# A gated feed-forward block beside a state-space block on one core: the last gate tiles as half products inside an output pair, and three differences by negated copy and DMA

## The chip, the core and the metric

The kernel runs on one core of a Trainium2 chip. The engines named here are PE (TensorE, matrix products; its weight loads are listed as PEld), DVE (VectorE), ACT (ScalarE), POOL (GpSimd, which here mostly issues transfers that add into their target) and SP (SyncE, which issues loads and stores). PE reads SBUF and writes PSUM; DVE and ACT read and write both. Each engine works through its own list of instructions in order and waits for the others by semaphores. The metric is the time of one execution on the device in microseconds (us); less is better.

## The reference

The input x has 2048 tokens of width 512. It is normalized per token, and the result is

```python
xn = _layernorm(x)
# A: a diagonal complex recurrence over the tokens, 512 states
h = Lam_bar[None, :] * h + Bu[:, t, :]                 # for t in 0..2047
y = 2.0 * jnp.einsum("blp,dp->bld", hseq, Cmat).real + xn * Dskip
# B: a gated feed-forward block, 512 -> 1792 -> 512
out_B = (silu(xn @ w1) * (xn @ w3)) @ w2
out = x + y + out_B
```

So there are three groups of matrix products: xn with w1 (gate) and w3 (up), xn with the state weights B, and a last one in which the products silu(gate)*up (1792 wide, 14 tiles of 128) and the states (real and imaginary, 8 tiles) meet w2 and C.

## The kernel before

**Blocks.** The 2048 tokens are four blocks of 512 (blocks 0 to 3). For each block the kernel makes the gate and up tiles (14 each, 128 features by 512 tokens), the state inputs (4 tiles, real and imaginary), rotates and scans the state inputs along the tokens on DVE (`ssm_tasks`: `pre_a`, `pre_b`, `pre_c`, then eight scans in two halves `hf`, then `post_a`, `post_b`, `post_c`), and writes gates and states as float16 into the tile `act`, which holds 22 tiles of 128 rows per token chunk. Where `pre_c` or `post_c` adds two large tiles, it either runs on DVE (L493, L525) or is an adding transfer that POOL issues (L495, L527).

**Output pairs.** `act` is multiplied with [w2; C] in eight output pairs, numbered 0 to 7; pair n belongs to block n // 2 and covers two chunks of 128 tokens. Each pair (`y_fast`, L1036) is a 2x2 block product by seven instead of eight half products (the scheme of Strassen and Winograd). Each half product is 11 matmuls of 128x256 (L1054). The left sides are a11, a12, a22 from `act` and four sums, S1 = a21 + a22, S3 = a11 - a21, S2 = S3 - a22 and S4 = a12 + S2, made ahead by `row_sums` (L993): S3 and S2 by DVE subtractions of 128x1408 (L1000), S1 by DVE or an adding transfer (L1005, L1007), S4 by DVE or a transfer inside the pair (L1093 to L1096). S2 and S3 of pair n live in `homes[n % 2]`. The half products of pairs 4, 5 and 6 run in the order 1, 4, 2, 6, 5, 7, 3; in pairs 4 and 5 the third is put off and runs inside the following pair after that one's product 5. `seeds(n)` loads a pair's PSUM tiles with the residual by ACT.

**Block 3's up side.** The same scheme is used on the up side of the last block (`glu_last`, L837): tiles 0 to 11 are three groups of four, each group seven half products of four 128x256 matmuls (`product`, L867), accumulated in four PSUM tiles g, e (pool `ps_y`), f, z (pool `ps_bu`), with copies between them by ACT (L857) and adds by DVE (L879). Its left sums come from `up_sums` (L834), and one of them, `s4n`, is made inside the group (L910). The gate side of these groups is done plainly, one tile at a time: four matmuls of 128x512 (`side`, L848) and a Silu on ACT (`gate_side`, L860). Tiles 12 and 13 are plain on both sides. After that come pairs 4 to 7; the pairs of block 3 are 6 and 7.

**Who sets the order.** The order is written out by hand. DVE's background work (scans, posts, sums) stands in a list `bg` (`Filler`, L24), which keeps an estimate of PE's and DVE's time; `bg.fill()` emits tasks from the head of the list as long as the estimate of DVE is not too far ahead of PE's, and `bg.flush(key)` emits everything from the head up to the last task with that key. POOL and SP issue their transfers in the order of the program.

Of the kernel before, what the change touches and what calls it, by code (L numbers as in the profile page):

```python
# [63 lines left out]
def kernel(  # L64
# [397 lines left out]
    def ssm_tasks(b, posts_last=False, between=(), middle=(), late=()):  # L462
# [5 lines left out]
        def half(hf):  # L468
            psl = slice(2 * hf, 2 * hf + 2)
            st = {}  # L470

            def pre_a():
                if b == 0:
                    sin_step((2 * hf + 1, 1))
                    nc.vector.tensor_scalar(out=tabe[:, psl, 2, :], in0=tabe[:, psl, 1, :], scalar1=-1.0,
                                            scalar2=None, op0=ALU.mult)
                st["g"] = u_blk[b, hf]
                if (b, hf) == (3, 0):
                    st["p"] = up.tile(FULL, BF16, name="u")
                elif b == NBLK - 1:  # L480
                    st["p"] = xtp.tile([P, NDT, TBLK], BF16, name="xnT").rearrange("p (j r) t -> p j r t", r=2)
                else:
                    st["p"] = ssmw.tile(FULL, BF16, name="p")
                nc.vector.tensor_tensor(out=st["p"][:, :, ::-1, :], in0=st["g"], in1=tabe[:, psl, 2:0:-1, :],
                                        op=ALU.mult)

            def pre_b():
                nc.vector.tensor_tensor(out=st["g"], in0=st["g"], in1=tabe[:, psl, 0:1, :].to_broadcast(FULL),  # L488
                                        op=ALU.mult)

            def pre_c():
                if b == 0 or (b, hf) == (2, 0):
                    nc.vector.tensor_tensor(out=st["g"], in0=st["g"], in1=st["p"], op=ALU.add)  # L493
                else:
                    gp.dma_start(out=st["g"], in_=st["p"], accum_op=ALU.add)  # L495

            def scan(j, ri):
                pt = 2 * hf + j
                init = 0.0
                if b in (1, 2):  # L500
                    init = ends[:, hf, 2 * j + ri:2 * j + ri + 1]
                elif b > 2:
                    init = act_blk[b - 1][:, CPB - 1, k_state(pt, ri), P - 1:P]
                v = st["g"][:, j, ri, :]
                nc.vector.tensor_tensor_scan(out=v, data0=rho[:, pt:pt + 1].to_broadcast([P, TBLK]), data1=v,  # L505
                                             initial=init, op0=ALU.mult, op1=ALU.add)

            def post_a(csl=slice(0, CPB)):
                if "p16" not in st:
                    st["p16"] = ssmw.tile(FULL, BF16, name="p").bitcast(FP16).rearrange(  # L510
                        "p j r (c t) -> p (j r c t)", t=P).rearrange("p (c k t) -> p c k t", c=CPB, t=P)
                tsl = slice(csl.start * P, csl.stop * P)
                nc.vector.tensor_tensor(out=by_state(st["p16"][:, csl]), in0=by_chunk(st["g"][:, :, ::-1, tsl]),  # L513
                                        in1=by_chunk(tabe[:, psl, 2:0:-1, tsl]), op=ALU.mult)

            def post_b(csl=slice(0, CPB)):
                tsl = slice(csl.start * P, csl.stop * P)
                n = csl.stop - csl.start
                nc.vector.tensor_tensor(out=by_state(act_state(b, hf)[:, csl]), in0=by_chunk(st["g"][:, :, :, tsl]),  # L519
                                        in1=by_chunk(tabe[:, psl, 0:1, tsl]).to_broadcast([P, 2, 2, n, P]), op=ALU.mult)  # L520
# [16 lines left out]
        transfers = (post0[2],) + (() if b == NBLK - 1 else (post1[2],)) + ((pre1[2],) if b > 0 else ()) + ((pre0[2],) if b in (1, 3) else ())  # L537

        def add(*fns):
            for fn in fns:  # L540
# [285 lines left out]
    def up_sums(b):  # L826
# [8 lines left out]
                for out, x, z, op in ((s1, a21, a22, ALU.add), (s3, a11, a21, ALU.subtract),  # L835
                                      (s2, s1, a11, ALU.subtract))]

    def glu_last(b):
        xnT = xnT_blk[b]
        s1, s2, s3, s4 = ups["s"]  # L840
# [33 lines left out]
        def halves(ps):  # L874
            return ps.rearrange("p (h t) -> p h t", h=2)

        def add(out, ps):
            bg.own(0.7)
            nc.vector.tensor_tensor(out=out, in0=halves(ps), in1=halves(s5), op=ALU.add)  # L879

        gates = []
        for f in range(4 * NG, NFT):
# [6 lines left out]
                gates.pop()()  # L889
            if f % 2 == 1:  # L890
                gates.append(lambda f=f, tiles=tiles: gate(f - 1, tiles))
        for n in range(NG):
            f0 = 4 * n
            a11, a12, a22, s1n, s2n, s3n, s4n = (v[:, :, n, :] for v in (
                up_quarter(0, 0), up_quarter(1, 0), up_quarter(1, 1), s1, s2, s3, s4))
            g, e = (ps_y.tile([P, TBLK], FP32, name="y_ps") for _ in range(2))
            f, z = (ps_bu.tile([P, TBLK], FP32, name="bu_ps") for _ in range(2))
            upper, lower = pair_tiles(), pair_tiles()
            product(g, a11, b11, True)
            copy(f, g)  # L900
            product(e, s1n, t1, True)
            copy(s5, e)
            gate_side(f0, upper[0])
            bg.fill(0.8)
            gates.pop()()
            product(f, a12, b21, False)
            product(g, s2n, t2, False)
            copy(e, g)
            bg.own(0.42)
            nc.vector.tensor_tensor(out=s4n, in0=a12, in1=s2n, op=ALU.subtract)  # L910
            copy(upper[1][:, :, 0:TH], halves(f))
            gate_side(f0 + 1, upper[0])
            bg.fill()
            product(g, s3n, t3, False)
            copy(z, g)
            add(lower[1][:, :, TH:TBLK], g)
            product(e, s4n, b22, False)
            add(upper[1][:, :, TH:TBLK], e)
            gate_side(f0 + 2, lower[0])
            bg.fill()  # L920
            gate(f0, upper)
            product(z, a22, t4, False)
            copy(lower[1][:, :, 0:TH], halves(z))
            gate_side(f0 + 3, lower[0])
            bg.fill()
            gates.append(lambda f0=f0, lower=lower: gate(f0 + 2, lower))
        seeds(4)
        return gates.pop()


    def res_list(b):
# [56 lines left out]
        return [[v[:, 0:n] for v in xs], [spare[:, 0:n], spare[:, n:2 * n]]], q  # L988

    sums = {}  # L990

    def row_sums(n, b, p):
        a = act(b)  # L993
        a11, a12 = a[:, 2 * p, 0:NK, :], a[:, 2 * p, NK:2 * NK, :]
        a21, a22 = a[:, 2 * p + 1, 0:NK, :], a[:, 2 * p + 1, NK:2 * NK, :]
        s3, s2 = (v.bitcast(FP16).rearrange("p (k t) -> p k t", t=P) for v in homes[n % 2])
        sums[n] = dict(a11=a11, a12=a12, a22=a22, s1=a21, s2=s2, s3=s3)

        def subtract(out, x, z):
            return lambda: nc.vector.tensor_tensor(out=out, in0=x, in1=z, op=ALU.subtract)  # L1000

        three = (0.84, subtract(s3, a11, a21), ("sums", n))
        two = (0.84, subtract(s2, s3, a22), ("sums", n))
        if n in (1, 6, 7):
# [31 lines left out]
    def y_fast(n, then=(), between=()):  # L1036
# [50 lines left out]
        def product2():  # L1087
# [9 lines left out]
            add(o1[:, D1], f, o1[:, D1])  # L1097
            if last:
                store(c1, o1, D1)
            if n + 1 < len(pairs) and n not in (1, 2, 3) and n - 1 not in LATER:  # L1100
                seeds(n + 1)
            steps()

# [43 lines left out]
        for i in ((1, 5, 2, 6, 4, 3, 7) if b == 0 else (1, 2, 4, 6, 5, 7, 3) if b == 1 else ORDER.get(n, (1, 4, 2, 6, 5, 7, 3))):  # L1147
# [10 lines left out]
            if between:  # L1158
# [2 lines left out]
                    bg.fill()  # L1161
                if n == 3 and not between:
                    bg.first(up_sums(3))
            if n == 2 and i == 7:
                seeds(3)

    ln_alloc(0)
    ln1a, ln1b = ln_tasks_vector(1)
# [70 lines left out]
    y_done.append(2)  # L1239
    y_fast(3, (), bu_fast(3, 1))  # L1240
    bg.flush("up")
    gate = glu_last(3)
    gate()
    for n in range(4, len(pairs)):
        ahead = row_sums(n + 1, *pairs[n + 1]) if n + 1 < len(pairs) else ()
# [37 lines left out]
```

## Time and profile before

| | |
|---|---|
| median of 3 runs | 201.05 us (200.91 to 201.06) |
| span of the profiled execution, first to last instruction | 199.5 us |
| PE busy | 195.6 us (98%) |
| DVE busy | 181.8 us (91%) |
| ACT busy | 135.0 us (68%) |
| POOL busy | 51.5 us (26%) |
| plain matmul 128x512 of block 3 (L848), 64 of them | 16 take 3.45 us |
| half product of four 128x256 matmuls (L869) | 0.44 us |
| DVE scan of 128x512 (L505), 32 of them | about 1.27 us |
| granted TensorE clock, mean | 0.999 |

The profiled execution's own time is its span of 199.5 us; the page gives no other time for it, and the median of the runs, which also counts what lies before the first and after the last instruction, is 1.55 us longer. A timeline row is: start in us, duration in us, engine, source line, operation, output and input tiles with their shapes, count, and in brackets how long the engine was idle before it and what ended that. Rows of engines that overlap consecutive instructions have durations a little longer than the distance to the next start; where a step follows a step on the same engine, the distance of the starts is what counts. In the table by stretches each pair after the interval is busy us and count of instructions by engine, then the granted clock, the share of the DMA engines and GB/s.

### The profile page before, as it was taken

Reading aid. Unit: us, or ns where it says so; the run is one execution under the profiler, and the core shown is the slowest. Engines: PE = TensorE matmul, PEld = TensorE weight load, DVE = VectorE, ACT = ScalarE, POOL = GpSimd, SP = SyncE. Lnnn points to the kernel's source line nnn. Section 1 sums busy time; section 2 is a strip of 40 time slices with the busy share of each in tenths; the row PEclk is TensorE's granted clock in tenths of the full one; section 3 lists DMA queues with packets and bytes.
Section 4 is the critical chain, followed back from the end, with each engine's and each line's share of the span. In section 5 each row is a group of like instructions: output and inputs, shape, how many; then the busy total and the mean of one; then the engine's idle time right before and its main releaser. Section 6 shows DMA issues by size and latency. Waiting matters only on the chain.

```text
span 199.5 us, 3700 instructions
## 1 busy us (share of the span) xinstructions
PE 195.6 (98%) x1401; PEld 130.7 (65%) x1401; DVE 181.8 (91%) x254; ACT 135.0 (68%) x281; POOL 51.5 (26%) x75
## 2 busy tenths in 40 slices
PE   8999999999999999999999999999999999999994
PEld 2774444444444488866555468888566678888893
DVE  3689699999999999989999997999999999999972
ACT  4699897699999996968998684362588783111220
POOL 7180289700411134041202305040021303310000
PEclk9999999999999999999999999999999999999999
DMA  4999996991497054730997455838137732941111
GB/s 138 326 277 200 302 186 124 343 273 23 69 181 141 0 105 82 135 105 0 156 148 119 89 92 98 172 83 132 53 59 129 149 56 52 174 92 36 53 44 40
DMA packets 32258, 25.12 MB, mean 126 GB/s; under 512 B 16240, under 2 KB 29936, under 8 KB 32240
## 3 DMA queue, kind: packets, MB, share of 16 engines
q0 software_dynamic: 6128, 11.38, 33.5%
q1 hardware_dynamic: 25536, 13.21, 26.8%
q10 hardware_dynamic: 576, 0.30, 0.5%
q8 instruction: 11, 0.18, 0.4%
q14 instruction: 7, 0.06, 0.1%
HBM read 7.74 MB, written 2.10 MB: 49 GB/s over the span
## 4 chain that ended last, share of the span: by engine, by line
PE 95%; DMA 2%; SPq 1%; issue 0%; DVE 0%
PE gu_ps L587 34%; PE gu_ps L1054 17%; PE y_ps L1054 10%; PE gu_ps L848 7%; PE bu_ps L1054 7%; PE bu_ps L454 3%; PE y_ps L454 3%; PE y_ps L869 3%; PE y_ps L780 3%; DMA w_sb<-in_B_w_dram 2%; PE gu_ps L619 2%; PE gu_ps L780 2%; PE bu_ps L869 1%; PE bu_ps L780 1%; PE bu_ps L619 1%; SPq L166 0%
## 5 line engine op out<-in xcount | busy, mean ns | idle before, releaser
L587 PE MATMUL gu_ps<-xnT,w_sb 128*128 128x512 bf16 x312 | 69.6, 379 | 0.0
L587 PEld LDWEIGHTS <-w_sb 128*128 128x128 bf16 x312 | 30.5, 98 | 34.2
L1054 PEld LDWEIGHTS <-act 128*128 128x128 f16 x462 | 43.5, 98 | 5.4
L596 ACT ACTIVATE g<-gu_ps 128x512 bf16<-128x512 f32 x41 | 24.8, 606 | 6.0 <-PE gu_ps L587 3.6
L597 ACT ACTIVATE u<-gu_ps 128x512 bf16<-128x512 f32 x41 | 24.8, 606 | 4.5 <-PE gu_ps L587 3.7
L505 DVE TENSOR_TENSOR_SCAN u<-rho,ends,u 128x512 bf16<-128x512 f32 x16 | 20.0, 1270 | 0.0
L527 POOL DMA_DIRECT2D act<-p x7 | 9.2, 1320 | 34.0 <-DVE act L519 22.1
L1054 PE MATMUL gu_ps<-w_sb,act 128*128 128x256 bf16 (+3 forms) x126 | 16.0, 267 | 0.0
L848 PE MATMUL gu_ps<-xnT,w_sb 128*128 128x512 bf16 x64 | 15.9, 379 | 0.0
L604 DVE TENSOR_TENSOR act<-g,u 128x1024 f16<-128x1024 bf16 x21 | 14.2, 679 | 0.4 <-ACT u L597 0.4
L860 ACT ACTIVATE g<-gu_ps 128x512 bf16<-128x512 f32 x14 | 8.4, 599 | 5.4 <-PE gu_ps L848 5.0
L454 PEld LDWEIGHTS <-bt 128*128 128x128 bf16 x64 | 6.3, 98 | 7.5
L1077 ACT ACTIVATE x_blk<-gu_ps 128x256 f32<-128x256 f32 (+1 forms) x9 | 3.3, 368 | 10.6 <-PE gu_ps L1054 10.6
L1054 PE MATMUL bu_ps<-w_sb,act 128*128 128x256 bf16 (+3 forms) x84 | 10.4, 264 | 0.0
L1054 PE MATMUL gu_ps<-ct,act 128*128 128x256 f16 (+1 forms) x72 | 10.4, 267 | 0.0
L848 PEld LDWEIGHTS <-w_sb 128*128 128x128 bf16 x64 | 6.3, 98 | 4.8
L505 DVE TENSOR_TENSOR_SCAN u<-rho,u 128x512 bf16<-128x512 f32 x8 | 9.2, 1206 | 0.0
L1054 PEld LDWEIGHTS <-x_blk 128*128 128x128 f16 x88 | 8.6, 98 | 1.0
L1054 PEld LDWEIGHTS <-tw 128*128 128x128 f16 x88 | 8.6, 98 | 1.0
L513 DVE TENSOR_TENSOR p<-u,tabe 128x2048 f16<-128x2048 bf16 (+1 forms) x8 | 8.7, 1085 | 0.1
L519 DVE TENSOR_TENSOR act<-u,tabe 128x2048 f16<-128x2048 bf16 (+1 forms) x8 | 8.7, 1083 | 0.0
L488 DVE TENSOR_TENSOR u<-u,tabe 128x2048 bf16<-128x2048 bf16 x7 | 8.5, 1219 | 0.1
(203 smaller groups left out, 392.5 us busy)
## 6 DMA issues: line engine op xcount, KB each, us to landing
act<-p POOLq DMA_DIRECT2D x6, 512.0 KB, 6.1
xn<-x_blk POOLq DMA_DIRECT2D x4, 512.0 KB, 5.5
out_dram<-xn SPq DMA_DIRECT2D x15, 128.0 KB, 1.7
w_sb<-in_B_w_dram SPq DMA_DIRECT2D x1, 1792.0 KB, 8.2
act<-act POOLq DMA_DIRECT2D x5, 352.0 KB, 4.6
w_sb<-in_B_w_dram SPq DMA_DIRECT2D x2, 768.0 KB, 6.4
u<-p POOLq DMA_DIRECT2D x3, 512.0 KB, 5.1
w_sb<-in_B_w_dram SPq DMA_DIRECT2D x4, 256.0 KB, 4.9
```

The source lines that it names most:

```text
L454: nc.tensor.matmul(out=ps, lhsT=bt[:, ri, dt, pt * P:(pt + 1) * P], rhs=xnT_blk[b][:, dt, :], start=(dt == 0), stop=(dt == NDT - 1))
L505: nc.vector.tensor_tensor_scan(out=v, data0=rho[:, pt:pt + 1].to_broadcast([P, TBLK]), data1=v, initial=init, op0=ALU.mult, op1=ALU.add)
L513: nc.vector.tensor_tensor(out=by_state(st["p16"][:, csl]), in0=by_chunk(st["g"][:, :, ::-1, tsl]), in1=by_chunk(tabe[:, psl, 2:0:-1, tsl]) ...
L519: nc.vector.tensor_tensor(out=by_state(act_state(b, hf)[:, csl]), in0=by_chunk(st["g"][:, :, :, tsl]), in1=by_chunk(tabe[:, psl, 0:1, tsl] ...
L527: gp.dma_start(out=a, in_=p16, accum_op=ALU.add)
L587: nc.tensor.matmul(out=ps[:, tsl], lhsT=w[:, dt, f * P:(f + 1) * P], rhs=xnT[:, dt, tsl], start=(dt == 0), stop=(dt == NDT - 1))
L596: nc.scalar.activation(out=g16[:, f % 2, :], in_=g_ps, func=ACT.Silu)
L597: nc.scalar.activation(out=u16[:, f % 2, :], in_=u_ps, func=ACT.Copy)
L604: nc.vector.tensor_tensor(out=act_gates(b, f - 1), in0=split(g16), in1=split(u16), op=ALU.mult)
L780: nc.tensor.matmul(out=out[:, h * TH:(h + 1) * TH], lhsT=left[:, h, k, :], rhs=right[:, k, :], start=(start and h == 0 and k == 0), stop=( ...
L848: nc.tensor.matmul(out=ps, lhsT=w[:, dt, f * P:(f + 1) * P], rhs=xnT[:, dt, :], start=(dt == 0), stop=(dt == NDT - 1))
L1054: nc.tensor.matmul(out=out, lhsT=left[:, k, :], rhs=right[k][:, cols], start=(start and k == 0), stop=(k == NK - 1), skip_group_check=True)
```

## The change

The change has four parts.

- **Gate side of the third group by half products.** The four gate tiles of tile group 2 of block 3 (tiles 8 to 11) are no longer made by `gate_side`, but by the same seven half products as the up side. The new function `group` makes the seven steps for either side; for the gate side (`gated`) the results go through Silu, and the two DVE adds write back to PSUM first. The left sums of the gate side are made by the new `gate_sums` from w1 into space that group 0's up sums held (three DVE operations on 128x512 elements, key "gs"), added to the end of the list `bg` after group 0.
- **Where it runs.** Groups 0 and 1 stay in the loop, with plain gate tiles. Steps one and five of group 2's up side and the gate product of group 1's lower half run before pair 4; everything else of group 2, both sides, runs between the half products of pair 4 (six lists, one after each of pair 4's products 1, 4, 2, 6, 5, 7). The first gate step flushes the key "gs". `seeds(5)` moves from pair 4's product 2 to the end of pair 4.
- **S3 of pairs 4 and 5 and S2 of pair 5.** These are no longer DVE subtractions. ACT writes the negated subtrahend (128x1408, L1083), and POOL issues a transfer that adds the minuend (L1084). The first (S3 of pair 4) stands before group 0, the second (S3 of pair 5) inside group 0, the third (S2 of pair 5) before pair 4.
- **Block 2's first half.** Its `pre_c` becomes an adding transfer (L495) instead of a DVE add of 128x2048 (L493).

```diff
@@ ssm_tasks @@
-                if b == 0 or (b, hf) == (2, 0):
+                if b == 0:
                     nc.vector.tensor_tensor(out=st["g"], in0=st["g"], in1=st["p"], op=ALU.add)
                 else:
                     gp.dma_start(out=st["g"], in_=st["p"], accum_op=ALU.add)
@@ new @@
+    def gate_sums():
+        s1, s2 = (ups["s"][i][:, :, 0, :] for i in range(2))
+        a11, a12, a21, a22 = (gate_quarter(*i) for i in ((0, 0), (1, 0), (0, 1), (1, 1)))
+        s3, s4 = gate_quarter(0, 1, True), gate_quarter(1, 0, True)
+        ups["gs"] = a11, a12, a22, s1, s2, s3, s4
+        return [(0.42, lambda out=out, x=x, z=z, op=op: nc.vector.tensor_tensor(out=out, in0=x, in1=z, op=op), "gs")
+                for out, x, z, op in ((s1, a21, a22, ALU.add), (s3, a11, a21, ALU.subtract),
+                                      (s2, s1, a11, ALU.subtract))]
@@ glu_last: the seven steps @@
+        def group(lefts, four, top, low, gated):
+            a11, a12, a22, s1n, s2n, s3n, s4n = lefts
+            g, e = (ps_y.tile([P, TBLK], FP32, name="y_ps") for _ in range(2))
+            f, z = (ps_bu.tile([P, TBLK], FP32, name="bu_ps") for _ in range(2))
+            def end(out, ps):
+                nc.scalar.activation(out=out, in_=halves(ps), func=ACT.Silu if gated else ACT.Copy)
+            def add(out, ps):
+                bg.own(0.7)
+                nc.vector.tensor_tensor(out=halves(ps) if gated else out, in0=halves(ps), in1=halves(s5), op=ALU.add)
+                if gated:
+                    end(out, ps)
+            def one():
+                product(g, a11, b11, True)
+                copy(f, g)
+            def five():
+                product(e, s1n, t1, True)
+                copy(s5, e)
+            def two():
+                product(f, a12, b21, False)
+            def six():
+                product(g, s2n, t2, False)
+                copy(e, g)
+                four()
+                end(top[:, :, 0:TH], f)
+            def seven():
+                product(g, s3n, t3, False)
+                copy(z, g)
+                add(low[:, :, TH:TBLK], g)
+            def three():
+                product(e, s4n, b22, False)
+                add(top[:, :, TH:TBLK], e)
+            def last():
+                product(z, a22, t4, False)
+                end(low[:, :, 0:TH], z)
+            return one, five, two, six, seven, three, last
@@ glu_last: the order @@
-        for n in range(NG):
+        by_copy[4][0]()
+        for n in range(NG - 1):
...
+            one()
+            five()
             gate_side(f0, upper[0])
             bg.fill(0.8)
             gates.pop()()
+            two()
+            six()
             gate_side(f0 + 1, upper[0])
             bg.fill()
+            if n == 0:
+                by_copy[5][0]()
+            seven()
+            three()
             gate_side(f0 + 2, lower[0])
             bg.fill()
             gate(f0, upper)
+            last()
             gate_side(f0 + 3, lower[0])
             bg.fill()
             gates.append(lambda f0=f0, lower=lower: gate(f0 + 2, lower))
+            if n == 0:
+                for t in gate_sums():
+                    bg.add(*t)
         seeds(4)
-        return gates.pop()
...
+        def gate_step(i):
+            def run():
+                if "steps" not in state:
+                    bg.flush("gs")
+                    right = ups["gs"]
+                    state["steps"] = group(right, lambda: sums4(right[6], right[1], right[4]), upper[0], lower[0], True)
+                state["steps"][i]()
+            return run
+        one, five, two, six, seven, three, last = up_steps
+        gone, gfive, gtwo, gsix, gseven, gthree, glast = (gate_step(i) for i in range(7))
+        first = gates.pop()
+        return (one, five, first, by_copy[5][1]), deque(((two, six), (seven, three), (last, gone, gfive), (gtwo, gsix),
+                                          (gseven, gthree), (glast, lambda: gate(f0, upper), lambda: gate(f0 + 2, lower))))
@@ row_sums @@
+        def from_copy(out, x, z):
+            nc.scalar.activation(out=out, in_=z, func=ACT.Copy, scale=-1.0)
+            gp.dma_start(out=out, in_=x, accum_op=ALU.add)
+        by_copy[n] = [lambda: from_copy(s3, a11, a21), lambda: from_copy(s2, s3, a22)]
         three = (0.84, subtract(s3, a11, a21), ("sums", n))
         two = (0.84, subtract(s2, s3, a22), ("sums", n))
+        if n in (4, 5):
+            three = (0.0, lambda: None, ("sums", n))
+        if n == 5:
+            two = (0.0, lambda: None, ("sums", n))
@@ y_fast @@
-            if n + 1 < len(pairs) and n not in (1, 2, 3) and n - 1 not in LATER:
+            if n + 1 < len(pairs) and n not in (1, 2, 3, 4) and n - 1 not in LATER:
                 seeds(n + 1)
...
-            if n == 2 and i == 7:
-                seeds(3)
+            if n in (2, 4) and i == 7:
+                seeds(n + 1)
@@ the end @@
-    gate = glu_last(3)
-    gate()
+    sums5 = row_sums(5, *pairs[5])
+    begin, beside = glu_last(3)
+    for step in begin:
+        step()
+        bg.fill()
...
-        y_fast(n, ahead if n == 4 else ())
+        y_fast(n, ahead if n == 4 else (), beside if n == 4 else ())
```

More of the change, by code (lines that the diff above doesn't have):

```diff
@@ L535, in ssm_tasks @@
         (pre0, scans0, post0), (pre1, scans1, post1) = (half(hf) for hf in range(NPT // 2))
-        transfers = (post0[2],) + (() if b == NBLK - 1 else (post1[2],)) + ((pre1[2],) if b > 0 else ()) + ((pre0[2],) if b in (1, 3) else ())
+        transfers = (post0[2],) + (() if b == NBLK - 1 else (post1[2],)) + ((pre1[2],) if b > 0 else ()) + ((pre0[2],) if b > 0 else ())
         def add(*fns):
@@ L836, in up_sums, with gate_quarter @@
                                       (s2, s1, a11, ALU.subtract))]
+    def gate_quarter(kh, r, half=False):
+        f0 = 4 * (NG - 1) * P
+        v = w1_sb[:, 2 * kh:2 * kh + 2, f0 + r * 2 * P:f0 + (r + 1) * 2 * P]
+        return v.bitcast(FP16) if half else v
+    def gate_sums():
[6 more added lines that the diff above has]
+                                      (s2, s1, a11, ALU.subtract))]
     def glu_last(b):
@@ L875, in halves, with sums4, up_lefts @@
             return ps.rearrange("p (h t) -> p h t", h=2)
-        def add(out, ps):
-            bg.own(0.7)
-            nc.vector.tensor_tensor(out=out, in0=halves(ps), in1=halves(s5), op=ALU.add)
+        def group(lefts, four, top, low, gated):
[33 more added lines that the diff above has]
+            return one, five, two, six, seven, three, last
+        def sums4(out, x, z):
+            bg.own(0.42)
+            nc.vector.tensor_tensor(out=out, in0=x, in1=z, op=ALU.subtract)
+        def up_lefts(n):
+            return [v[:, :, n, :] for v in (up_quarter(0, 0), up_quarter(1, 0), up_quarter(1, 1), s1, s2, s3, s4)]
         gates = []
@@ L891, in glu_last @@
                 gates.append(lambda f=f, tiles=tiles: gate(f - 1, tiles))
-        for n in range(NG):
+        by_copy[4][0]()
+        for n in range(NG - 1):
             f0 = 4 * n
[L894 to L897, printed above, removed]
+            lefts = up_lefts(n)
             upper, lower = pair_tiles(), pair_tiles()
[L899 to L902, printed above, removed]
+            one, five, two, six, seven, three, last = group(
+                lefts, lambda: sums4(lefts[6], lefts[1], lefts[4]), upper[1], lower[1], False)
+            one()
+            five()
             gate_side(f0, upper[0])
@@ L905, in glu_last @@
             gates.pop()()
[L906 to L911, printed above, removed]
+            two()
+            six()
             gate_side(f0 + 1, upper[0])
             bg.fill()
[L914 to L918, printed above, removed]
+            if n == 0:
+                by_copy[5][0]()
+            seven()
+            three()
             gate_side(f0 + 2, lower[0])
@@ L921, in glu_last @@
             gate(f0, upper)
-            product(z, a22, t4, False)
-            copy(lower[1][:, :, 0:TH], halves(z))
+            last()
             gate_side(f0 + 3, lower[0])
@@ L926, in glu_last @@
             gates.append(lambda f0=f0, lower=lower: gate(f0 + 2, lower))
+            if n == 0:
+                for t in gate_sums():
+                    bg.add(*t)
         seeds(4)
-        return gates.pop()
+        f0 = 4 * (NG - 1)
+        upper, lower = pair_tiles(), pair_tiles()
+        lefts = up_lefts(NG - 1)
+        up_steps = group(lefts, lambda: sums4(lefts[6], lefts[1], lefts[4]), upper[1], lower[1], False)
+        state = {}
+        def gate_step(i):
[11 more added lines that the diff above has]
+                                          (gseven, gthree), (glast, lambda: gate(f0, upper), lambda: gate(f0 + 2, lower))))
     def res_list(b):
@@ L990 @@
     sums = {}
+    by_copy = {}
     def row_sums(n, b, p):
@@ L1241 @@
     bg.flush("up")
-    gate = glu_last(3)
-    gate()
+    sums5 = row_sums(5, *pairs[5])
[3 more added lines that the diff above has]
+        bg.fill()
     for n in range(4, len(pairs)):
-        ahead = row_sums(n + 1, *pairs[n + 1]) if n + 1 < len(pairs) else ()
+        ahead = (sums5 if n == 4 else row_sums(n + 1, *pairs[n + 1])) if n + 1 < len(pairs) else ()
         if n > 4:
```

## The prediction

> **What bounds the kernel now.** I read the page first: span, busy shares, chain.
>
> ```profile
> span 199.5 us, 3700 instructions
> PE 195.6 (98%) x1401; PEld 130.7 (65%) x1401; DVE 181.8 (91%) x254; ACT 135.0 (68%) x281; POOL 51.5 (26%) x75
> PE 95%; DMA 2%; SPq 1%; issue 0%; DVE 0%
> ```
>
> The chain that ended last is TensorE (PE) for 95% of the span, so every wait put into PE's stream lengthens the run by its full length, and work taken off another engine gives nothing. Then the busy time by stretches from block 3's feed-forward part on (PE, PEld, DVE, ACT, POOL):
>
> ```profile
> 140.00:150.00 10.00, 10.00 (x63) 5.90 (x61) 9.50 (x13) 7.15 (x13) 1.28 (x1) 1.00 0.32 61
> 150.00:160.00 10.00, 10.00 (x70) 6.62 (x68) 9.69 (x14) 8.29 (x16) 2.60 (x3) 1.00 0.77 140
> 160.00:170.00 10.00, 10.00 (x86) 8.19 (x84) 9.73 (x14) 5.32 (x13) 1.72 (x2) 1.00 0.29 54
> 170.00:180.00 10.00, 10.00 (x94) 8.97 (x93) 9.73 (x14) 1.77 (x6) 2.12 (x2) 1.00 0.69 129
> ```
>
> PE never rests, but VectorE (DVE) has only 0.3 to 0.5 us free in each 10, and ScalarE (ACT) is well filled in the groups before 160. Hence both small slacks decide. The timeline of the first tile group gives ACT's:
>
> ```profile
> 145.07 0.60 PE L869 MATMUL bu_ps<-xnT,w_sb 128*128 128x256 bf16 x4
> 148.56 0.60 PE L869 MATMUL bu_ps<-x_blk,w_sb 128*128 128x256 f16 x4
> ...
> 143.54 0.60 ACT L857 ACTIVATE u<-gu_ps 128x512 bf16<-128x512 f32 x1 [0.27 <-PE gu_ps L848]
> 144.03 0.59 ACT L857 ACTIVATE bu_ps<-y_ps 128x512 f32<-128x512 f32 x1
> 147.64 0.62 ACT L857 ACTIVATE bu_ps<-y_ps 128x512 f32<-128x512 f32 x1
> ```
>
> The copy g to f ends at 144.62 and product two, which adds onto f, starts at 145.07; the copy g to z ends at 148.26 and the last product starts at 148.56. From other pairs a successor starts some 0.06 after the copy, so the slacks are 0.39 and 0.24 us. DVE's timeline gives the prices of the scans and posts:
>
> ```profile
> 166.74 0.42 DVE L1065 TENSOR_TENSOR xn<-gu_ps,xn 128x256 bf16<-128x256 f32 x1 [0.23 <-PE gu_ps L1054]
> ...
> 169.08 0.69 DVE L513 TENSOR_TENSOR p<-u,tabe 128x1024 f16<-128x1024 bf16 x1
> 169.68 0.68 DVE L519 TENSOR_TENSOR act<-u,tabe 128x1024 f16<-128x1024 bf16 x1
> ...
> 171.02 3.63 DVE L505 TENSOR_TENSOR_SCAN x_blk<-rho,act,x_blk 128x512 bf16<-128x512 f32 x3
> ```
>
> Next starts come 0.1 before the shown end: 0.34 for a 128x256 add, 0.60 for a post, 1.18 for a scan.
>
> **Work removed and added.** PE: 16 matmuls of 128x512 (group of 16: 3.45 us) become 28 of 128x256 (0.437 for four: 3.06). Gain 0.39, the only certain one. DVE loses three 128x1408 subtractions (0.81 each by start to start) and block 2's 128x2048 add (1.14), and gains three gate sums and S4 (0.34 each for 512 elements) and two adds that now go PSUM to PSUM (bounded by the 128x512 PSUM adds, 0.61, and twice that; I take 0.61). Net about -1. Since PE waits for DVE nowhere before, that is worth 0.
>
> **Block 2's add as a DMA.** POOL issues it (0.9 to 1.5 us of POOL) near 107.7; the 512 KB transfers like it landed in 5.1. Its first scan ran at 121.6, so about 8 us cover it: 0. It stands ahead of the residual's DMA on POOL, which is read tens of us later: 0.
>
> **Three negated copies on ACT.** No row has 128x1408. Bounds: not under a 128x512 copy (0.60), not over 2.75 times the slowest 128x512 row, the normalizing one (805 ns): 2.2. Nearest are immediate-scale copies, 0.38 at 256 and 0.60 at 512, or 0.86 ns per element: 1.37, with 0.1 of overlap 1.26 of ACT.
> First copy: ACT's order puts it between the up side of tile 13 and group 0's copy to f. Its input, block 2's first states, is sent about 1.2 us earlier than before and landed by 141, so it starts at 144.03; copy f moves from 144.03 to about 145.29. Product two must wait: 1.26 - 0.39 = 0.87.
> Second copy: between the gate activation of tile f0+1 and the copy to z; the last product waits 1.26 - 0.24 = 1.02. ACT then has pauses again, so both stay: **1.9** (with 0.60 instead, about 0.4; with 2.2, 3.7).
> Third copy: behind the copies of the third group's products; the copy of the sixth product is late by about 0.15 at seven: 0.15.
> Behind the second copy DVE suffers too: its add of the seventh product waits for that copy to z, so DVE stands from about 148.1 to 150.4, with 2048-wide products, gates, S2 and scans queued behind.
> POOL sends each copy's add in the order of the code: the first before block 3's u transfer, whose own cause ends later (148.1); the second before the x_blk transfer (cause near 155.6); the third before the row sum S1 of pair 5. The scan that needs u comes at about 156.2, u lands near 148.2 + 0.9 + 4.5: 0. The 352 KB adds (4.6) are first read by DVE's S2 of pair 4 some 4 us after landing and by pair 4's seventh product 25 us later: 0. SP's stores stay in their order: 0.
>
> **Third group beside pair 4.** Putting group 2 behind the DVE pause, I get DVE's scans ending at 163.4 and its S4 at 163.8, while product three could start at 163.07: 0.83. With 0.05 at five and the 0.15 above: **1.0**. If DVE had kept its lead this is 0; if its pause were a us longer, 2.
>
> **The gate sums.** This decides. They are added at the end of DVE's task list, with the key "gs"; the first gate step, after product 2 of pair 4, flushes that key, so everything ahead is emitted first. DVE's order then is: pair 4's add of product 2, post multiplications, four scans, two post multiplications and an add, and only then the sums. PE's order has after product 2: last, gate one, gate five (which reads the first sum), and product 6 behind it. The add cannot start before product 2 ends (+0.2 after its issue). From there DVE needs 0.34 + 1.2 + 4 x 1.18 + 0.1 + 1.8 + 0.42 = 8.6; PE has two half products, 0.87. Wait: 8.6 + 0.2 - 0.87 = **7.95**. All terms have rows; ends 7.5 and 8.5.
>
> **PE after that wait.** PE pauses nowhere for over 1 us once it has begun. The only row after rest is the first:
>
> ```profile
> 0.76 4.16 PE L196 MATMUL bu_ps<-const-bfloat16-1.0 128*128 128x512 bf16 x10 [0.76 <-PEq L1267]
> ```
>
> Ten matmuls take 4.16 where ten later ones take 2.16, though the granted clock reads 1.00 there. Bounds: 0 (only the start is slow) and 4 (slow for twice as long). I take **2.0**, as PE comes from rest in both.
> [...] No row of this trace shows a fall in mid-run.
>
> **End of the gate group.** Pair 5's first product now takes the PSUM buffer of the gate's e, free only after three's end, the DVE add behind seven's, two Silu steps: about 0.75 after the last gate product; **0.75** (0 to 1.5). Seeds of pair 5 and the gates to act come behind; pair 6 reads them some 10 us later: 0. The scans and posts are done early then, so pairs 5 to 7 lose nothing and gain nothing.
>
> **Sum** against the profiled span of 199.5: -0.4 + 1.9 + 1.0 + 7.95 + 2.0 + 0.75 = +13.2, 212.7. The runs' median, 201.05, lies 1.55 above the span: **214.2**.
>
> **Rivals.**
> Clock kept: PE resumes at full pace; 212.2. For it: the clock column reads 1.00 throughout. Against: the first row.
> Copies covered: ACT takes the two copies without delaying f and z, and DVE keeps its lead: less 1.9 and some 0.5 of the next term, 211.8. Against: 0.39 and 0.24 of slack under any copy over 0.7.
> Longer recovery: half pace for about 8 us, or DVE's scans late for a transfer: +2, 216.2.
> The other side: the saved matmuls count because DVE has the first gate sum when gate five comes. Then, with copies and clock at their lower ends, 201.05 - 0.39 = 200.7. It decides at one point: the sums would have to come 7.95 us earlier, so the scans before them must be done by product 2 of pair 4. DVE's order excludes it unless those scans finish before that product's add, which stands ahead of them.
>
> **How the numbers follow.** Forecast 0.60 (own range 213 to 215.5), clock kept 0.18, copies covered 0.06, longer recovery 0.13, other side 0.03. A measurement here tells from no change what differs by over 0.2%, 0.4 us. From 211.5 to 216.5 holds all but the far part of the longer recovery and the other side, over 8 in 10. Faster 0.02, same 0.01 (the other side split), slower 0.97.
>
> **What would show it.** In the profile after: a PE gap of about 8 us near 166.5 to 174.5, released by DVE's first gate sum; four scans in a row on DVE inside it; matmuls of 128x256 at double spacing for about 4 us behind it; gaps near 145 and 149.4 of about 1 us released by ACT; copies of 1.3 to 1.4 us; a gap under 1 us before pair 5. Wrong would be: no long gap (the order read wrongly), or an equally long one released by a DMA.

## The result and the profile after

| | before | after |
|---|---|---|
| median of 6 runs | 201.06 us (200.86 to 201.74) | 216.13 us (215.01 to 216.61) |
| span of the profiled execution | 199.5 us | 214.1 us |
| mean granted TensorE clock | 0.999 | 0.976 |

The changed kernel takes 1.0735 times the time of before (95% interval 1.0709 to 1.0761), 15.1 us more. The forecast was 214.2. One of the nine runs of the last version below took 295.0 us at a mean granted clock of 0.756 and is left out of that version's ratio. The page of the kernel after, with the same lines as shown of before:

```profile
span 214.1 us, 3736 instructions
...
PE 198.1 (93%) x1400; PEld 133.2 (62%) x1413; DVE 181.5 (85%) x256; ACT 140.5 (66%) x288; POOL 55.4 (26%) x79
...
PE 16%; DVE 8%; issue 7%; DMA 4%; POOL 1%; ACT 1%; POOLq 0%; DVEq 0%; ACTq 0%
```

PE is busy 93% instead of 98%. Its busy time grew by 2.5 us although it has less to do: part of its work ran slower. The chain, 95% PE before, now has DVE, DMA, POOL and ACT in it (the shares shown add up to 37% only, so it was followed through part of the span). The waits of PE (what waited, for which engine and line, us in total, times, longest) give the names:

```profile
PE y_ps L883 <- DVE bt L848: 8.0, 1, 8.0
PE bu_ps L883 <- ACT bu_ps L871: 1.8, 2, 1.1
PE y_ps L883 <- DVE w_sb L939: 0.9, 1, 0.9
...
PE y_ps L1143 <- ACT g L897: 0.6, 1, 0.6
PE bu_ps L1143 <- DMA act<-tw: 0.4, 1, 0.4
```

In the order of these lines: the gate sum that gate five reads, ACT's copies to f and z in group 0, S4 of the third group, the last Silu ahead of pair 5, and a transfer at pair 3. The first four were in the forecast, the fifth was not. The same stretches as before (PE, PEld, DVE, ACT, POOL, then clock, DMA share, GB/s):

```profile
140.00:150.00 10.00, 9.18 (x56) 5.47 (x56) 7.88 (x10) 7.52 (x12) 3.06 (x3) 1.00 0.39 71
150.00:160.00 10.00, 8.95 (x59) 5.84 (x60) 8.80 (x12) 8.38 (x17) 2.60 (x3) 1.00 1.05 191
160.00:170.00 10.00, 6.57 (x59) 5.39 (x57) 9.38 (x13) 5.59 (x11) 3.78 (x4) 1.00 0.77 139
170.00:180.00 10.00, 4.59 (x22) 3.28 (x23) 6.78 (x11) 0.60 (x1) 0.00 (x0) 0.50 0.20 29
```

From 170 to 180 PE ran 22 matmuls where it ran 94 before, at half the granted clock. The timeline of PE around the waits (start, duration, and in brackets the idle time and its releaser):

```profile
146.50 0.60 PE L883 MATMUL bu_ps<-xnT,w_sb 128*128 128x256 bf16 x4 [0.70 <-ACT bu_ps L871]
...
150.99 0.60 PE L883 MATMUL bu_ps<-x_blk,w_sb 128*128 128x256 f16 x4 [1.06 <-ACT bu_ps L871]
...
164.77 0.61 PE L883 MATMUL y_ps<-xnT,w_sb 128*128 128x256 bf16 x4 [0.89 <-DVE w_sb L939]
...
166.86 0.60 PE L883 MATMUL y_ps<-xnT,w_sb 128*128 128x256 bf16 x4
175.41 1.03 PE L883 MATMUL y_ps<-x_blk,bt 128*128 128x256 f16 x4 [7.95 <-DVE bt L848]
176.24 2.56 PE L1143 MATMUL gu_ps<-tw,x_blk 128*128 128x256 f16 x11
...
184.76 0.92 PE L1143 MATMUL y_ps<-w_sb,act 128*128 128x256 bf16 x7 [0.62 <-ACT g L897]
```

Gate one is issued until 167.30 (0.44 after its start); gate five starts 8.1 us later. The 11 matmuls at 176.24 take 2.56 us; before, 11 like them took 1.36. What DVE and ACT did meanwhile:

```profile
144.59 1.37 ACT L1083 ACTIVATE x_blk<-act 128x1408 f16<-128x1408 f16 x1
149.07 1.39 ACT L1083 ACTIVATE tw<-act 128x1408 f16<-128x1408 f16 x1
...
150.97 1.29 DVE L901 TENSOR_TENSOR u<-y_ps,bt 128x512 bf16<-128x512 f32 x2 [2.28 <-ACT bu_ps L871]
168.17 4.80 DVE L505 TENSOR_TENSOR_SCAN x_blk<-rho,act,x_blk 128x512 bf16<-128x512 f32 x4
174.94 0.42 DVE L848 TENSOR_TENSOR bt<-w_sb 128x512 f16<-128x512 bf16 x1
```

Two post multiplications, the four scans, and behind them two more post multiplications and an add, stand between pair 4's add of product 2 (166.62) and the first gate sum, which PE waits for; DVE rests for less than 0.1 us in all that.

### The profile page after: what moved, and what is told of

The parts are those of the page before. It is cut to its first block, busy times and chain, and to the rows that moved or that the text cites. A ratio compares the mean times of both kernels' runs of the same rounds, so it can differ in the third digit from the quotient of the medians.

```text
span 214.1 us, 3736 instructions
## 1 busy us (share of the span) xinstructions
PE 198.1 (93%) x1400; PEld 133.2 (62%) x1413; DVE 181.5 (85%) x256; ACT 140.5 (66%) x288; POOL 55.4 (26%) x79
## 5 line engine op out<-in xcount | busy, mean ns | idle before, releaser
L587 PE MATMUL gu_ps<-xnT,w_sb 128*128 128x512 bf16 x304 | 68.9, 379 | 0.4
L587 PEld LDWEIGHTS <-w_sb 128*128 128x128 bf16 x312 | 30.5, 98 | 34.2
L596 ACT ACTIVATE g<-gu_ps 128x512 bf16<-128x512 f32 x41 | 24.8, 605 | 6.1 <-PE gu_ps L587 3.2
L883 PE MATMUL y_ps<-x_blk,bt 128*128 128x256 f16 x32 | 5.6, 306 | 8.0 <-DVE bt L848 8.0
L883 PEld LDWEIGHTS <-w_sb 128*128 128x128 bf16 (+1 forms) x80 | 7.9, 100 | 6.3 <-issue 2.4
L862 PE MATMUL gu_ps<-xnT,w_sb 128*128 128x512 bf16 x45 | 11.5, 379 | 0.1
L1143 PEld LDWEIGHTS <-x_blk 128*128 128x128 f16 x88 | 9.2, 105 | 1.6
L1143 PE MATMUL gu_ps<-tw,x_blk 128*128 128x256 f16 x66 | 9.4, 297 | 0.0
L883 PEld LDWEIGHTS <-bt 128*128 128x128 f16 x32 | 3.4, 108 | 9.0 <-DVE bt L848 8.2
L874 ACT ACTIVATE g<-gu_ps 128x512 bf16<-128x512 f32 x10 | 6.0, 599 | 4.5 <-PE gu_ps L862 4.3
```

The source lines that it names most:

```text
L587: nc.tensor.matmul(out=ps[:, tsl], lhsT=w[:, dt, f * P:(f + 1) * P], rhs=xnT[:, dt, tsl], start=(dt == 0), stop=(dt == NDT - 1))
L596: nc.scalar.activation(out=g16[:, f % 2, :], in_=g_ps, func=ACT.Silu)
L862: nc.tensor.matmul(out=ps, lhsT=w[:, dt, f * P:(f + 1) * P], rhs=xnT[:, dt, :], start=(dt == 0), stop=(dt == NDT - 1))
L874: nc.scalar.activation(out=g16[:, f % 2, :], in_=side(w1_sb, f), func=ACT.Silu)
L883: nc.tensor.matmul(out=out[:, h * TH:(h + 1) * TH], lhsT=left[:, k, h * P:(h + 1) * P], rhs=right[:, k, :], start=(start and h == 0 and k ...
L1143: nc.tensor.matmul(out=out, lhsT=left[:, k, :], rhs=right[k][:, cols], start=(start and k == 0), stop=(k == NK - 1), skip_group_check=True)
```

## The experiments

All of them do the whole computation. Each ratio is to runs of the kernel before on the same chip, whose medians were 201.1 to 201.2 us.

**The gate sums first.** The sums go to the head of DVE's list instead of its end.

```diff
-                for t in gate_sums():
-                    bg.add(*t)
+                bg.first(gate_sums())
```

> The changed kernel with one edit: the three sums of the gate side go to the head of DVE's task list instead of its end, so no scans stand ahead of them. Theory (the order of the list makes the long wait): the 8.0 us wait at gate five is gone, and with it the slow matmuls behind it (2.35 us by their rows); 216.1 - 8.1 - 2.35 = 205.7, with the waits on ACT in group 0 (0.9 and 1.0), at pair 3's last product (0.4 to 0.6) and ahead of pair 5 (0.6 to 1.5) still there; 205 to 206.8. Rival (DVE simply has too much work in this stretch, whatever the order): the wait moves to another product of pairs 4 to 6, and the time stays above 211.

Measured: 206.07 us, ratio 1.0262 (1.0227 to 1.0297). So 10.1 us of the 15.1 hang on the place of three operations of 0.4 us in a list. PE does not wait for them any more, and the half-speed stretch behind that wait is gone (mean clock 0.999). S4 of the third group is later instead (DVE starts it at 164.98 instead of 164.32), and DVE has the three sums ahead of it; in PE's timeline of this kernel:

```profile
165.44 0.61 PE L883 MATMUL y_ps<-xnT,w_sb 128*128 128x256 bf16 x4 [1.77 <-DVE w_sb L939]
```

**PE kept busy through the wait.** 33 matmuls of 128x512 on constants, into the gate's tile z, which is overwritten later, stand between gate one and gate five (the trace has records of 32).

```diff
+                if i == 1:
+                    zt = state["steps"][7]
+                    for _ in range(33):
+                        nc.tensor.matmul(out=zt, lhsT=ones[:, 0:P], rhs=ones[:, 0:TBLK], start=True, stop=True, ...)
```

> The changed kernel with 33 matmuls of 128x512 on constants put into PE's stream between gate one and gate five, into a PSUM tile that is overwritten later; they take 33 x 0.216 = 7.1 us and fit into the 8.0 us that PE waits there anyway. Theory (rest slows PE): gate five still starts near 175.4, the matmuls after it come at 0.109 us each and the granted clock stays 1.00; 216.1 - 2.35 = 213.8, from 213.4 to 214.2. Rival (the double spacing after the wait comes from weight loads or data that arrive slowly, not from rest): spacing stays at 0.21 and the time at 216.

Measured: 213.52 us, ratio 1.0613 (1.0593 to 1.0632), mean clock 1.0; 2.6 us less than the change, with 7 us more work on PE. In PE's timeline of this kernel:

```profile
167.24 7.38 PE L998 MATMUL bu_ps<-const-bfloat16-1.0 128*128 128x512 bf16 x32 [0.30 <-ACT u L897]
174.90 0.61 PE L883 MATMUL y_ps<-x_blk,bt 128*128 128x256 f16 x4 [0.28 <-DVE bt L848]
```

Gate five comes only 0.5 us earlier than in the change (PE's first plain matmuls of block 0 were 0.5 earlier already, 12.34 instead of 12.88), and the matmuls behind it run at full pace (11 of 128x256 in 1.36 us instead of 2.56): from gate five to the last instruction it takes 36.4 us instead of 38.7, 2.3 less. So the loss behind the wait is of PE's rest, and not of data that comes late.

**The copies early.** Both S3 copies stand ahead of tile 12 instead of in front of and in group 0.

```diff
+        by_copy[4][0]()
+        by_copy[5][0]()
         gates = []
...
-        by_copy[4][0]()
         for n in range(NG - 1):
...
-            if n == 0:
-                by_copy[5][0]()
```

> The changed kernel with the two negated copies of S3 (pairs 4 and 5) moved ahead of feed-forward tile 12, where ACT is idle for 3.2 us, instead of before and inside group 0. Theory (ACT's order makes the two waits of 0.9 and 1.1 us in group 0): both waits go, DVE's idle 2.3 us behind the second goes too and with it the 1 us wait at the third group's product three; 216.1 - 1.9 - 1.0 = 213.2, from 212.6 to 214.4; the 8 us wait stays, since it begins with pair 4's product 2. Rival (ACT is short of time over the whole stretch): waits of about 2 us appear elsewhere in groups 0 and 1, 216.

Measured: 213.41 us, ratio 1.0601 (1.058 to 1.0622), 2.7 us less than the change. The two waits for ACT's copies to f and z are gone, and the wait for S4 fell from 0.89 to 0.37; the one for the gate sum stayed at 7.96.

**The copies alone**, in the kernel before, at the places that the change gives them: S3 of pairs 4 and 5 by `from_copy`, the rest as before.

```diff
+        if n in (4, 5):
+            three = (0.0, lambda: None, ("sums", n))
...
+        by_copy[4][0]()
         for n in range(NG):
...
+            if n == 0:
+                by_copy[5][0]()
```

> The kernel before with one part of the change alone: S3 of pairs 4 and 5 by negated copy and adding transfer, the copies at the changed kernel's places (ahead of group 0 and inside it); everything else as before. Theory (a copy of 1.37 us on ACT against slacks of 0.39 and 0.24 us): PE waits 0.9 and 1.0 us for ACT in group 0 and nowhere else; 201.2 + 1.9 = 203.1, from 202.6 to 203.8. Rival (the two subtractions taken off DVE pay for it): 201.2 within 0.4.

Measured: 203.2 us, ratio 1.0109 (1.0093 to 1.0124). In its timeline product two starts 0.87 and the last product 1.01 us later than the matmuls ahead of them allow, the same gaps as in the change. A third delay was not expected: product seven of the third group starts 0.28 us late (161.63), behind ACT's copy of product six, which ends at 161.58; why that copy comes late was not settled.

**Block 2's add as a transfer alone**, in the kernel before.

```diff
-                if b == 0 or (b, hf) == (2, 0):
+                if b == 0:
...
-... + ((pre0[2],) if b in (1, 3) else ())
+... + ((pre0[2],) if b > 0 else ())
```

> The kernel before with one part of the change alone: block 2's first addition as an adding transfer instead of on DVE. Theory (DVE, relieved of 1.1 us, sends block 2's first states earlier, so that their 512 KB go out on POOL ahead of pair 3's S4, which lands late): pair 3's last product waits 0.4 to 0.6 us; 201.06 + 0.5 = 201.6, from 201.3 to 201.8. Rival (the late landing in the changed kernel came from its other transfers): no wait at pair 3, 201.06 within 0.1, or a little less through DVE's relief.

Measured: 201.54 us, ratio 1.0024 (1.0011 to 1.0036). The wait at pair 3 is there with this part alone. POOL's timeline of the kernel before, and then POOL's and PE's of this one:

```profile
132.16 0.86 POOL L1093 DMA_DIRECT2D act<-tw  x1 [8.85 <-PE bu_ps L1054]
132.93 1.41 POOL L527 DMA_DIRECT2D act<-p  x1
```

```profile
131.65 1.29 POOL L527 DMA_DIRECT2D act<-p  x1 [9.44 <-PE bu_ps L1054]
132.41 1.45 POOL L1093 DMA_DIRECT2D act<-tw  x1
...
139.01 0.94 PE L1054 MATMUL bu_ps<-w_sb,act 128*128 128x256 bf16 x7 [0.39 <-DMA act<-tw]
```

Before, pair 3's S4 (act<-tw, 352 KB) was issued first. With 1.1 us less on DVE the list emits the post multiplications of block 2's first half earlier (the second ran at 129.87 instead of 131.41), and with them their transfer (act<-p, 512 KB), which now stands ahead of S4 on POOL.

**The same, with those two transfers in the old order.** The transfer of the posts is held until S4 has been issued; nothing else differs from the run above.

```diff
+                elif (b, hf) == (2, 0) and "released" not in held_posts:
+                    held_posts.append(lambda: gp.dma_start(out=a, in_=p16, accum_op=ALU.add))
                 else:
                     gp.dma_start(out=a, in_=p16, accum_op=ALU.add)
...
                 gp.dma_start(out=v["s4"], in_=v["s2"], accum_op=ALU.add)
+                if n == 3:
+                    for fn in held_posts:
+                        fn()
+                    held_posts.append("released")
```

> The kernel before with block 2's first add as a transfer only, but with the transfer of block 2's first-half posts (act<-p, 512 KB) held until pair 3's S4 transfer (act<-tw, 352 KB) has been issued, so that the two stand on POOL's queue in the order they have in the kernel before. Theory (the order of these two transfers on POOL makes the wait of 0.39 at pair 3's last product, not the added transfer itself): no wait of PE on act<-tw, 201.0 to 201.3 us, equal to the kernel before (201.1 to 201.2) within 0.2%. Rival (the added traffic makes the S4 transfer land late whatever the order): the wait of 0.4 stays, 201.5 us as with the order changed.

Measured: 200.98 us, just under the forecast, ratio 0.9995 (0.9985 to 1.0004), and PE no longer waits for S4. So the order on POOL is the cause, and not the added traffic. This is the lowest median of all kernels here, but not apart from before.

**Three mends together**: sums first, copies early, block 2's add back on DVE.

> The changed kernel with three edits: the gate sums at the head of DVE's list, the two S3 copies ahead of feed-forward tile 12, and block 2's first addition back on DVE. Theory (the waits found are separate and add up): 206.1 - 1.9 (copies) - 0.5 (pair 3's transfer) = 203.7, less up to 0.9 as DVE reaches product three of the third group earlier; 202.6 to 203.8, with waits left at product three and ahead of pair 5. Rival (the waits hide each other): above 204.5.

Measured: 206.77 us, ratio 1.0292 (1.0261 to 1.0323): the three gains don't add, and the forecast of 202.6 to 203.8 missed; the rival's time, above 204.5, was right. PE's and DVE's timeline of this kernel:

```profile
163.87 0.92 PE L883 MATMUL y_ps<-xnT,w_sb 128*128 128x256 bf16 x4 [2.91 <-DVE w_sb L939]
...
158.69 4.80 DVE L505 TENSOR_TENSOR_SCAN u<-rho,act,u 128x512 bf16<-128x512 f32 x4
163.41 0.40 DVE L939 TENSOR_TENSOR w_sb<-w_sb,bt 128x512 f16<-128x512 bf16 x1
```

Against the sums first alone, PE could start product three 2.7 us sooner (160.80 instead of 163.51), but DVE starts S4 only 1.6 us sooner (163.41 instead of 164.98), behind four scans in a row; the wait for S4, 1.77 there, is 2.91. And the clock falls again, which neither the theory nor the rival had: the 27 matmuls from 163.87 on take 4.62 us instead of 2.95, with the clock at 0.50 from 164.03 to 167.44.

**Six mends**: besides the three, the S1 and scan tasks that pair 4's start pulls out go behind its product 4; less lead for DVE's list ahead of product three; and pair 5's tiles g and z swapped.

```diff
-        if p == 0 and b > 1:
+        if p == 0 and b > 1 and n != 4:
             bg.flush(("scan", b + 1))
...
-            if b > 0:
+            if b > 0 and n != 4:
                 bg.first(list(then))
...
-            bg.fill()
+            bg.fill(-0.5 if n == 4 else None)
...
+                if n == 4 and i == 4:
+                    bg.flush(("scan", 3))
+                    bg.first(list(then))
...
+            if n == 5:
+                g, z = z, g
```

> The last kernel with two more edits: pair 5's PSUM tiles g and z change places, so that its first product takes the tile of the gate's g instead of that of e; and the scans of block 3's first half are put behind product 4 of pair 4 (before, pair 4's start sends all four of them out ahead of the third group's S4), with less background work let ahead in between. Theory: the waits at product three (0.4 to 1.8) and ahead of pair 5 (0.6) go, and what is left is the work saved on PE, 0.4: 200.8 to 201.6 against 201.2. Rival (DVE cannot hold the work of this stretch): waits of over 1 us appear at pair 5 or 6, released by DVE, 202.5 and more.

Measured: 201.78 us, ratio 1.0034 (1.0021 to 1.0047), a little over the forecast of 200.8 to 201.6. The span falls by 4.6 us against the three mends: 2.91 of wait and 1.67 of half pace. In this part of PE's timeline one wait is left, 0.62 us ahead of pair 5 (170.45) for the gate's last Silu, and a short delay of 0.30 at product seven of the third group.

The swap did nothing: with and without it pair 5 starts some 0.06 us after the second of the two Silu ends (170.40 here, 175.00 with the three mends). Why it waits for the second either way was not settled, nor which of the two other edits ended the wait for S4.

**Everything of the change, in order**: six mends, with block 2's add as a transfer again and POOL's order held.

> The version with all the mends before, with block 2's first add given back to a transfer as in the change, and the same two transfers of POOL in the order of the kernel before: so it holds every part of the change, and undoes only what the parts did to the order of other work. Theory (of the change's 15 us nothing is left but PE's wait of 0.62 ahead of pair 5 for the gate's last Silu; VectorE's 1.1 us less are off the path): 201.6 to 201.9 us, 0.3% above the kernel before. Rival one (VectorE's relief moves its list and with it a new wait for an S4 or a gate sum): above 202.2. Rival two (the relief lets the gate's last adds, and so the Silu ahead of pair 5, come sooner): 201.1 or less.

Measured: 201.66 us, ratio 1.0029 (1.0014 to 1.0043). The starts of group 0 and of pair 5 on PE, in the kernel before and then in this one:

```profile
143.34 0.60 PE L869 MATMUL y_ps<-xnT,w_sb 128*128 128x256 bf16 x4
170.14 0.93 PE L1054 MATMUL y_ps<-w_sb,act 128*128 128x256 bf16 x7
```

```profile
142.81 0.60 PE L887 MATMUL y_ps<-xnT,w_sb 128*128 128x256 bf16 x4
170.27 0.93 PE L1147 MATMUL y_ps<-w_sb,act 128*128 128x256 bf16 x7 [0.61 <-ACT g L901]
```

This execution was 0.53 us ahead from its start: the first plain matmuls of block 0, where the two kernels are the same, begin at 12.35 instead of 12.88. So the distance between the two rows is what counts, 27.46 us against 26.80, 0.66 more. Pair 5 starts 0.78 later than the matmul ahead of it allows. Product seven of the third group starts 0.30 late (160.32): ACT's third negated copy stands ahead of the copy of product six, which ends at 160.27. Without these two the distance would be 0.42 shorter than before. That is the saved work (forecast 0.39), and it is less than what the two delays cost. No version here beats the kernel before.

## Why the prediction was right, and where not

The time lay 1.9 us above the forecast, inside the range of 211.5 to 216.5 but outside the 213 to 215.5 of the forecast's own case. By the number alone the rival of a longer recovery (216.2) would fit best; the trace shows that the likeliest case held, and that the missing 1.9 us are several small terms. Step by step, in starts of PE's timeline (in both profiles block 0's first plain matmuls begin at 12.88, so the starts compare directly):

| step | forecast | measured |
|---|---|---|
| work saved | -0.4 | -0.42 (the version in order) |
| block 2's add as a DMA | 0 | 0.57 |
| three negated copies, group 0 | 1.9 | 0.87 + 1.01 = 1.88 |
| third group beside pair 4 | 1.0 | 0.16 + 0.16 + 1.04 = 1.36 |
| gate sums | 7.95 | 8.1 (wait 7.95) |
| PE after that wait | 2.0 | 2.35 |
| end of the gate group | 0.75 | 0.78 |
| sum, and the move of the span | 13.2 | 14.62 of 14.6 |
| outside the span | 1.55 | 2.03 |

**Block 2's add as a DMA** is the step that was wrong in kind. I asked whether its own 8 us of cover would hold, and whether the residual's DMA behind it on POOL would suffer, and put 0. Both held. What I did not follow is that the engine it was taken from comes earlier with everything after it, transfers too. The prediction even says, under the first copy, that block 2's first states are sent about 1.2 us earlier (they went 1.06 earlier, at 131.87), but not what this transfer overtakes on POOL. Pair 3's last product started at 139.23 in the change, 0.57 later than its predecessors allow. The two runs of that part, alone and with POOL's order held, show it.

**Three negated copies.** The copy took 1.37 to 1.39 us (forecast 1.37 from the slope of the narrower rows), and 0.39 and 0.24 of slack were read rightly from two starts each. DVE's stand of 2.28 us behind the second copy was forecast as 148.1 to 150.4 and came at 148.7 to 151.0. The third copy's 0.15 at product seven did not show in the change, while five of the other versions, the one in order among them, have 0.30 there.

**Third group beside pair 4.** Products one and five start 0.16 late each (158.98 and 159.58), right behind DVE's two adds for the group before; product three starts 1.04 late, as DVE starts S4 at 164.32 and not at the forecast 163.4. The mechanism held, and the size was 0.36 low.

**The gate sums.** The working by order of emission held to 0.2 us. The sums-first run shows that the order alone made it. (That PE waits for DVE nowhere before is not quite so: it waits 0.16 us at 5.08, in the start, which has no weight here.)

**PE after that wait.** The mechanism was right, the size 0.35 low: the 23 matmuls from 175.41 to 180.27 took 4.86 us where 2.51 is full pace. The rows of the clock, PE alone in stretches of 1 us (busy, clock, DMA share, GB/s):

```profile
169.00:170.00 1.00, 0.00 (x0) 0.99 1.17 208
170.00:171.00 1.00, 0.00 (x0) 0.50 0.81 117
...
179.00:180.00 1.00, 1.00 (x7) 0.50 0.00 0
180.00:181.00 1.00, 1.00 (x10) 0.89 0.00 0
```

The clock halves at 169.99, 2.5 us into the rest, and comes back at 180.23, 4.8 us after work resumed: a slow stretch of 10.24 us, with 4.8 us of work at half pace at its end. The six runs fall into two groups, four at 216.1 to 216.6 with a mean clock of 0.976 and two at 215.0 to 215.2 with 0.983. At half clock, 0.017 of 213 us lost would be an estimated 7 us of slow stretch instead of 10.24; only one of the six, at 0.976, has a trace.

The three mends show it a second time: there the clock halves at 164.03, 3.07 us after a rest of 2.91 us began, and comes back at 167.44, 3.57 us after work resumed, a slow stretch of 3.41 us. With the copies early, where the rest is 7.96 us, the mean clock of 0.976 over 211.6 us gives an estimated 10.2 us at half clock, as in the change. What sets the length of a slow stretch was not shown. The forecast of 2.0 us came from the kernel's first row, ten matmuls in 4.16 us instead of 2.16; here 4.8 us of work ran at half pace and lost 2.35.

**Outside the span.** The 1.55 was the median of other runs less one span. Later runs of the kernel before have 1.72 to 1.93 between their own time and span, those of the change 1.96 to 2.04. So up to half of the 0.5 was a poor reading. The rest stays open: keeping PE busy left it (1.98 to 2.06), the early copies did not (1.75 to 1.77).

**The rivals.** *Clock kept* fell by the clock rows and by the run with PE kept busy (2.6 us less in the medians, 2.3 behind gate five in the traces). *Copies covered* fell by the copies alone, 1.1% slower. *Longer recovery* was wrong in size: 2.35 us lost, not 4. *The other side* did not come even with every wait but one mended: the sums first still left 2.6%, all in order 0.3%. The 0.4 us that the change saves is less than the delays of 0.78 and 0.30 that stay there.

## What to carry to other kernels

Where a flush pulls out a list up to a key, the price of a short task at the end is everything queued ahead of it, and the order of emission, summed by the rows of the engine, gave that price to 0.2 us here. A long wait on PE can cost more than its length: here 8.1 + 2.35 us, and 2.91 + 1.67 with the three mends. When an engine is relieved, ask which transfers are now emitted earlier and what they overtake on a shared queue; and when several waits are mended, expect the next engine in line to set the pace, since here the gains of single mends did not add. Before two profiles are compared by their starts, check a point ahead of the change: here it moved by up to 0.5 us between executions.

## What was not expected of the hardware

- A rest of 2.9 us (the three mends) already halved the clock, for 3.41 us that began only 0.16 us after work had resumed. One of 1.8 us (the sums first) did not in the profiled run; of its other three runs two had a clock of 1.0 at 205.9 and 206.0 us, one 0.992 at 207.7, the mean clock that the three mends have with their 3.41 us, but it has no trace.
- In the change transfers into SBUF that overlapped landed later than their like before. Pair 3's S4 of 352 KB landed 6.6 us after its issue, behind the posts' 512 KB (3.8 as the median of such before). The 352 KB of the two S3 transfers took 6.7 and 8.0 us (act<-act of that size 4.6 before), the 512 KB of u<-u 8.0 instead of 4.5; the scan that reads u waited 0.19 us for it at 157.06, where the prediction had no wait.
- In the first matmuls of the kernel PE runs at half pace (ten of 128x512 take 4.16 us, later 2.16) with the column of the clock at 1.00; in mid-run the column shows 0.50. The trace of the kernel before has its first entry of the clock, at full, 4.5 us after the first instruction (6.1 in the change), and ahead of it the column shows 1.00. A clock of 1.00 at the start is no evidence for full pace there.
